# ScalarE's addition in the linear attention's queries: queued with the reduction, or as an item of its own

## The chip, the cores and the metric

The kernel runs on one core of a Trainium2 chip. A core has five engines, each with an in-order queue of its own: TensorE (PE; its weight loads, PEld, overlap its matmuls), VectorE (DVE), ScalarE (ACT), GpSimd (POOL) and SyncE (SP, which issues the DMAs here). They wait for one another by semaphores. An instruction that waits also holds whatever stands behind it on its engine. The metric is the device time of one execution in microseconds (us), the median of the runs shown.

## The reference

Two attention blocks on the same input x (2048 tokens, 1024 columns, 32 heads of 32 columns), mixed by a gate. Block A is linear attention, block B softmax attention:

```python
phi = lambda t: jnp.where(t > 0, t + 1, jnp.exp(t)) + 1e-6
pq, pk = phi(q), phi(k)                       # block A
kv = jnp.einsum("bhsd,bhse->bhde", pk, v)
z = jnp.einsum("bhsd->bhd", pk)
num = jnp.einsum("bhqd,bhde->bhqe", pq, kv)
den = jnp.einsum("bhqd,bhd->bhq", pq, z)[..., None] + 1e-6
a = (num / den) @ wo
...
p = _softmax(q @ k * Dh ** -0.5)              # block B, per head
b = (p @ v) @ wo
...
g = _sigmoid((x * gate_w).sum(-1, keepdims=True))
return g * a + (1 - g) * b
```

The constant 1e-6 that is added to `den` is the subject of the change.

## The kernel before, in words

All products in float32 are made of three matmuls of a high and a low part (lines 147 to 149). After a first phase that computes block B's values, queries and keys, four streams share the engines. They are Python generators, and a planner in the kernel's source runs them and so writes out the order of every engine's queue by hand:

- `maxima` (block B): for each head, 64 score tiles of 128 x 512 on PE (L890), whose row maxima VectorE takes (L895); at a head's end these are turned into two rows (`mh`, `ml`) and stored by DMA beside the head's queries.
- `heads_` (block B): the scores again, transposed (L1041), their exponentials on ScalarE (L1045), their product with the values on PE in groups of 5, 5 and 6 tiles (L1139), and their sums on GpSimd (L1092, L1088) and VectorE (L1099, L1101). L943 and L950 to L953 end a head.
- `linear` (block A): units of 128 tokens by 512 columns, 24 matmuls each (L147 to L149), in the order values (of block B), keys and values, queries, output product. The queries have two chunks of 16 units, so 32 units.
- `output`: the last products, the gate and the mixture.

The planner keeps a clock for each engine, `T["pe"]`, `T["act"]`, `T["dve"]`, `T["pool"]`. `use(engine, cost, *after)` moves an engine's clock to the latest of its own time and the times given, adds a planned cost, and returns the end with a latency. An instruction is put into its engine's queue at the moment at which the planner runs the Python line, so the order of these calls is the order of the queue. VectorE's work is mostly deferred: `defer` makes an item with a due time `at`, and `fill(until)` runs those that fit before `until`, which reaches 0.4 us, or, between score tiles, 1.2 us, past PE's planned time. `run` computes an item's planned end before it calls the item's function with that end. `take()` gives out one of six PSUM banks and runs the deferred readers that still hold it. `tasks` is a list of pairs (start, function): in each round of the main loop the first task whose start is no later than PE's planned time is run ahead of the streams.

A unit of the queries: after its matmuls, ScalarE makes the exponential, the positive part and a sum (`phi`, L567 to L569). Then a chain of four items on VectorE: `sums` (L799) and `scaled` (L802, times the keys' sums `zrep`), `dens` (L807, a reduction over each head's 32 columns to the 128 x 16 tile `dn`) and `divide` (L812 a reciprocal, L813 the product with it). `dens` also issues ScalarE's addition of the constant to `dn` (L808) and sets the due time of `divide`, which is `last[0]`. After `divide` a task, `queries`, transposes the result on PE (L693), ScalarE copies it rounded (L695), VectorE takes the remainder (L698) and two DMAs store both (`oA`, L700), on SP's queue, where the loads of later rows (`xs`, L562) and of block B's heads (L861) stand as well.

Of the kernel before, what the change touches and what calls it, by code (L numbers as in the profile page):

```python
# [46 lines left out]
def kernel(  # L47
# [19 lines left out]
    nc = tc.nc  # L67
# [39 lines left out]
    eps = sb.tile([P, 1], F32, name="eps")  # L107
# [47 lines left out]
    def use(eng, cost, *after):  # L155

        T[eng] = max(T[eng], *after, 0.0) + cost
        return T[eng] + LATENCY[eng]
# [35 lines left out]
    def ended(items, *also):  # L194

        if any(item.end is None for item in items):
            return None
        return max([0.0, *also] + [item.end for item in items])
# [19 lines left out]
    def take():  # L218

        idle = [b for b in RING if not held[b]]  # L220
        times = {b: ended(readers[b], free[b]) for b in idle}
        b = min(idle, key=lambda b: (times[b] is None, times[b] or 0.0))
        need(readers[b])
        free[b] = ended(readers[b], free[b])
        readers[b].clear()
        held[b] = True
        return b
# [77 lines left out]
    def xop(name, p, i):  # L305
        return big[XO[name][p]][:, i * C:(i + 1) * C]
# [126 lines left out]
    for np_, js in enumerate(PAIRS):  # L433
# [4 lines left out]
        for pos, k in enumerate(KORDER):  # L438
# [3 lines left out]
            for t in range(2 * TPC):  # L442
# [3 lines left out]
                ps = bank[t]  # L446
# [14 lines left out]
        for g in range(NK):  # L461
            nxt = pair_ops(g + 1) if g + 1 < NK else None
            for q, name in enumerate(PRODUCTS):
                ps = bank[used % 8]
# [165 lines left out]
    def load_mix():  # L630
        while stores:
            stores.popleft()()
        a, c = mix_todo.popleft()
        for i in range(HK):
            nc.sync.dma_start(mix_hi[i], a_wo[(a * HK + i) * P:(a * HK + i + 1) * P, c * C:(c + 1) * C])
        mix_here.append((a, c, T["pe"] + MIX_LAND))
# [70 lines left out]
    def linear():  # L707
        extra = iter(())
        coming_w = deque()
        for n, (i, t) in enumerate(units):  # L710
            kind, c = chunks[i]
            pos = n % NT
            here_ = n < NT // 2
            follow = chunks[i + 1] if i + 1 < len(chunks) else None
            xp = xp_t[n % 2]
            yield bank_at
            b = take()
            ps = bank[b]
            T["pe"] = max(T["pe"], free[b])
            lin_kind[0] = kind  # L720
            if kind in ("q", "o") and c == 0 and t in (2, 8, NT - 2):
                yield lambda: None if mix_here else 0.0
                if t < NT - 2:
                    load_mix()
                while stores:
                    stores.popleft()()
            if n < 2:
                load_head(n)
                load_v(n)
            for k in range(NK):  # L730
                yield lambda: ended(w_left[k], w_ready[k], 0.0 if here_ else xp_ready[n % 2])
                need(w_left[k])
                if here_:
                    jj, tt = divmod(n, TPC)
                    stat = [xop(PLACE[jj][k // HK], p, k % HK)[:, tt * P:(tt + 1) * P] for p in range(2)]
                else:
                    stat = [blocks(xp, p)[:, k] for p in range(2)]
                for m, _ in enumerate(three(ps, stat, (wpart(k, 0), wpart(k, 1)), k)):
                    lin_pe(1.0)
                    if m < 2:  # L740
                        yield always
                if k == 0 and n + 7 == len(units) and not o_main[0]:
                    load_o(0)
                if k == 1 and n + 1 == len(units):
                    split_o(0, slice(0, NK - 1))
                if k == NK // 2 and n + 1 == len(units) and over["head"]:
                    split_o(1, slice(0, NK - 1))
                if k == NK - 1:
                    yield from extra
                if follow and follow[0] == "o":  # L750
                    if pos == NT - 1:
                        w_left[k].clear()
                        yield lambda: 0.0 if mixed.count((k // HK, follow[1])) == 8 else None
                        load_wa(follow[1], k)
                    continue
                if kind == "v":
                    if pos == (NT - 4 if k < NK // 2 else NT - 3):
                        coming_w.append(load_w(*follow, k, LEAD_W + 1, first_raws[k]))
                elif follow and pos == NT - 2 and k < min(LEAD_W, NK):
                    coming_w.append(load_w(*follow, k, LEAD_W + 1))  # L760
                if follow and pos == NT - 1:
                    split_w(*follow, k, *coming_w.popleft(), nc.vector if kind == "v" else nc.gpsimd)
                    if kind != "v" and k + LEAD_W < NK:
                        coming_w.append(load_w(*follow, k + LEAD_W, LEAD_W + 1))
            if NT // 2 <= n + 2 < len(units):
                load_xp(n + 2)
            extra = iter(())
            e, r = mid[3 + n % 3], mid[6]
            if kind == "v":
                give(b, use("act", 0.5, T["pe"] + LATENCY["pe"]))  # L770
                v_out(c, t, ps, mid[(10, 11, 7, 8, 9)[n % 5]])
            elif kind == "kv":
                va = mid[7][:, (n % 2) * HC:(n % 2 + 1) * HC]
                yield from keys_alone(n - 2)
                nc.scalar.copy(va, ps[:, HC:])
                use("act", 0.28, T["pe"] + LATENCY["pe"])
                end = phi(ps, e, HC)

                def more(end, c=c, t=t, e=e, ps=ps):
                    pk = e[:, :HC]  # L780
                    nc.vector.scalar_tensor_tensor(pk, pk, 1.0, ps[:, :HC], op0=ALU.min, op1=ALU.add)
                    z_end[c % 2] = use("pool", 0.69, end)
                    if t == 0:
                        nc.gpsimd.tensor_copy(zsum[c % 2], pk)
                    else:
                        nc.gpsimd.tensor_add(zsum[c % 2], zsum[c % 2], pk)

                todo = [defer(more, end, 0.34)]
                give(b, 0.0, todo)
                keys(n, c, t, e, va, todo)  # L790
                if t == NT - 1:
                    extra = keysum(c)
            elif kind == "q":
                yield lambda: None if n - 3 not in turned and chunks[units[n - 3][0]][0] == "q" else 0.0
                end = phi(ps, e, C)
                d = dn[n % 2]

                def sums(_, e=e, ps=ps):
                    nc.vector.scalar_tensor_tensor(ps, e, 1.0, ps, op0=ALU.min, op1=ALU.add)  # L799

                def scaled(_, c=c, ps=ps, r=r):
                    nc.vector.tensor_mul(r, ps, zrep[:, c * C:(c + 1) * C])  # L802

                last = []

                def dens(end, r=r, d=d, last=last):
                    nc.vector.tensor_reduce(d, r.rearrange("p (h d) -> p h d", d=DH), AX.X, ALU.add)  # L807
                    nc.scalar.add(d, d, eps)  # L808
                    last[0].at = use("act", 0.2, end)

                def divide(_, t=t, e=e, ps=ps, d=d):
                    nc.vector.reciprocal(d, d)  # L812
                    nc.vector.tensor_mul(  # L813
                        e.rearrange("p (h d) -> p h d", d=DH), ps.rearrange("p (h d) -> p h d", d=DH),
                        d.unsqueeze(2).to_broadcast([P, C // DH, DH]))

                todo = chain(((sums, 0.63), (scaled, 0.63), (dens, 0.63), (divide, 0.9)), end)
                last.append(todo[-1])
                give(b, 0.0, todo)
                tasks.append((lambda todo=todo: both(ended(todo + o_left), bank_at()),  # L820
                              lambda n=n, c=c, t=t, e=e, todo=todo: queries(n, c, t, e, todo)))
            else:
                res = mid[14 if c == 0 and t < TPC else (14, 8)[n % 2]]
                give(b, use("act", 0.5, T["pe"] + LATENCY["pe"]))
                nc.scalar.copy(res, ps)
                nc.sync.dma_start(ra_d[t][:, c * C:(c + 1) * C], res)
        over["lin"] = True
        load_all()
# [9 lines left out]
    tasks = []  # L838
# [25 lines left out]
    def load_head(h):  # L864
        load_q(h)
        for j in range(NJ):
            load_k(h, j)
# [4 lines left out]
    def load_v(h):  # L872
        c, o = divmod(h * DH, C)
        nc.sync.dma_start(v_tile(h), v_d[c][:, :, o:o + DH])
# [537 lines left out]
```

## Time and profile before

| | |
|---|---|
| median of 3 runs | 2850.99 us (2850.79 to 2853.78) |
| the profiled execution | 2850.77 us, of it 2849.0 us span from first to last instruction |
| busy: PE, weight loads, VectorE, ScalarE, GpSimd | 100%, 71%, 79%, 57%, 65% of the span |
| mean granted TensorE clock | 0.999 |
| the queries' additions (L808) | 32, from 1722.4 to 2133.9 us |

The times of the trace are counted from the first instruction. PE's records are those of pipelined matmuls with modelled ends, so they overlap, and a PE that is shown as busy may still pause briefly: the distance from start to start tells more. An idle time is put down to the event that ended it, and idle time of an engine that is not the bottleneck costs nothing.

### The profile page before, as it was taken

Reading aid. Unit: us, or ns where it says so; the run is one execution under the profiler, and the core shown is the slowest. Engines: PE = TensorE matmul, PEld = TensorE weight load, DVE = VectorE, ACT = ScalarE, POOL = GpSimd, SP = SyncE. Lnnn points to the kernel's source line nnn. Section 1 sums busy time; section 2 is a strip of 40 time slices with the busy share of each in tenths; the row PEclk is TensorE's granted clock in tenths of the full one; section 3 lists DMA queues with packets and bytes.
Section 4 is the critical chain, followed back from the end, with each engine's and each line's share of the span. In section 5 each row is a group of like instructions: output and inputs, shape, how many; then the busy total and the mean of one; then the engine's idle time right before and its main releaser. Section 6 shows DMA issues by size and latency. Waiting matters only on the chain.

```text
span 2849.0 us, 44413 instructions
## 1 busy us (share of the span) xinstructions
PE 2836.9 (100%) x15744; PEld 2033.4 (71%) x15744; DVE 2238.1 (79%) x3775; ACT 1617.8 (57%) x3007; POOL 1854.5 (65%) x646
## 2 busy tenths in 40 slices
PE   9999999999999999999999999999999999999999
PEld 7888888766666666666666667676766666666787
DVE  6666656888888888888888888888988778886743
ACT  5334320666666667666666666675656566656421
POOL 1212220778898889988988888687778777875000
PEclk9999999999999999999999999999999999999999
DMA  5956865432333223332323234574464444424663
GB/s 166 295 170 207 263 192 165 125 94 92 109 90 93 90 89 110 93 103 90 122 79 93 90 119 149 182 219 141 145 199 140 125 141 136 141 85 147 220 213 105
DMA packets 302498, 400.57 MB, mean 141 GB/s; under 512 B 92682, under 2 KB 185354, under 8 KB 299146
## 3 DMA queue, kind: packets, MB, share of 16 engines
q1 hardware_dynamic: 302276, 397.73, 45.3%
q8 instruction: 124, 2.03, 0.3%
q14 instruction: 98, 0.80, 0.1%
HBM read 287.57 MB, written 108.79 MB: 139 GB/s over the span
## 4 chain that ended last, share of the span: by engine, by line
PE 95%; DMA 2%; DVE 2%; issue 1%; ACT 1%; POOL 0%; SPq 0%; POOLq 0%; ACTq 0%
PE bank L1041 17%; PE bank L890 16%; PE bank L1139 15%; PE bank L147 11%; PE bank L149 11%; PE bank L148 11%; PE bank L410 3%; PE bank L409 3%; PE bank L408 3%; PE bank L943 1%; DMA mid<-in_xT 1%; PE bank L693 1%; PE bank L449 1%; PE bank L448 1%; PE bank L447 1%
## 5 line engine op out<-in xcount | busy, mean ns | idle before, releaser
L1092 POOL TENSOR_TENSOR big<-big,big 128x1536 f32<-128x1536 f32 (+1 forms) x434 | 1557.2, 3588 | 184.6 <-ACT big L1045 162.2
L895 DVE TENSOR_REDUCE mx<-bank 128x1 f32<-128x512 f32 x2048 | 1311.1, 681 | 315.5 <-PE bank L890 311.3
L1045 ACT ACTIVATE big<-bank 128x512 f32<-128x512 f32 x2048 | 1181.2, 601 | 517.5 <-PE bank L1041 449.5
L1041 PE MATMUL bank<-big,big 128*128 128x512 f32 x2048 | 808.9, 397 | 2.4 <-DMA big<-ml 2.3
L890 PE MATMUL bank<-big,big 128*128 128x512 f32 x2048 | 802.4, 392 | 0.3 <-ACT big L1045 0.3
L147 PE MATMUL bank<-big,big 128*128 128x512 f32 x1408 | 551.7, 392 | 2.9 <-ACT big L253 1.7
L149 PE MATMUL bank<-big,big 128*128 128x512 f32 x1408 | 550.1, 391 | 0.7 <-DVE big L254 0.4
L148 PE MATMUL bank<-big,big 128*128 128x512 f32 x1408 | 550.3, 391 | 0.0
L1041 PEld LDWEIGHTS bank<-big,big 128*128 128x128 f32 x2048 | 383.8, 188 | 158.5 <-issue 64.7
L1139 PE MATMUL bank<-big,mid 128*32 128x512 f32 x4096 | 460.8, 595 | 0.0
L890 PEld LDWEIGHTS bank<-big,big 128*128 128x128 f32 x2048 | 384.6, 188 | 84.5 <-ACT big L1045 4.3
L1139 PEld LDWEIGHTS bank<-big,mid 128*32 128x32 f32 x4096 | 127.8, 110 | 265.2 <-issue 265.2
L147 PEld LDWEIGHTS bank<-big,big 128*128 128x128 f32 x1408 | 264.3, 188 | 66.1 <-ACT big L1045 5.9
L149 PEld LDWEIGHTS bank<-big,big 128*128 128x128 f32 x1408 | 264.3, 188 | 57.5 <-DVE big L254 0.8
L148 PEld LDWEIGHTS bank<-big,big 128*128 128x128 f32 x1408 | 264.4, 188 | 55.2
L1101 DVE TENSOR_TENSOR bank<-bank,big 128x512 f32<-128x512 f32 (+1 forms) x434 | 280.5, 646 | 6.8 <-ACT big L1045 5.5
L1088 POOL TENSOR_TENSOR big<-big,big 128x1536 f32<-128x1536 f32 (+1 forms) x31 | 111.6, 3602 | 235.6 <-ACT big L1045 123.7
L254 DVE TENSOR_TENSOR big<-mid,big 128x512 fp32r<-128x512 f32 x216 | 153.2, 732 | 84.1 <-ACT big L253 84.0
L387 POOL TENSOR_TENSOR mid<-mid,mid 128x512 f32<-128x512 f32 x16 | 20.7, 1291 | 277.6 <-DVE big L254 266.3
L253 ACT CAST big<-mid 128x512 fp32r<-128x512 f32 x216 | 130.2, 624 | 97.9 <-POOL mid L388 54.5
L410 PE MATMUL bank<-big,big 128*128 128x512 f32 x448 | 174.4, 389 | 0.1
L408 PE MATMUL bank<-big,big 128*128 128x512 f32 x448 | 174.4, 389 | 0.0
(103 smaller groups left out, 1977.3 us busy)
## 6 DMA issues: line engine op xcount, KB each, us to landing
big<-xs SPq DMA_DIRECT2D x208, 512.0 KB
qk<-mid SPq DMA_DIRECT2D x128, 256.0 KB
big<-oA SPq DMA_DIRECT2D x64, 512.0 KB
big<-qk SPq DMA_DIRECT2D x96, 256.0 KB
big<-qk SPq DMA_DIRECT2D x384, 64.0 KB
mid<-in_b_wqkv SPq DMA_DIRECT2D x88, 256.0 KB
xs<-big SPq DMA_DIRECT2D x64, 256.0 KB
oA<-mid SPq DMA_DIRECT2D x64, 256.0 KB
```

The lines of the kernel that those rows point to most:

```text
L147: yield nc.tensor.matmul(ps, sh, mh_, start=(kt == 0), stop=False)
L148: yield nc.tensor.matmul(ps, sh, ml_, start=False, stop=False)
L149: yield nc.tensor.matmul(ps, sl, mh_, start=False, stop=(kt == NK - 1))
L408: nc.tensor.matmul(ps, sh, mh_, start=(i == 0), stop=False)
L410: nc.tensor.matmul(ps, sl, mh_, start=False, stop=(i == HK - 1))
L890: nc.tensor.matmul(bank[b], q[:, t * P:(t + 1) * P], k[:, j * C:(j + 1) * C], start=True, stop=True)
L895: nc.vector.tensor_reduce(m[:, t, j:j + 1], bank[b], AX.X, ALU.max)
L1041: nc.tensor.matmul(bank[b], k[:, t * P:(t + 1) * P], q[:, j * C:(j + 1) * C], start=True, stop=True)
L1045: nc.scalar.activation(pr_t[i][:, j * C:(j + 1) * C], bank[b], AF.Exp, scale=SCALE)
L1092: nc.gpsimd.tensor_add(lacc[:, :qp], lacc[:, :qp], pr(t)[:, :qp])
L1101: nc.vector.tensor_add(lacc[:, qp:] if t == NT - 1 else l_b[:, :n], l_b[:, :n], src)
L1139: nc.tensor.matmul(av_b[j * DH:(j + 1) * DH, :], v[:, t, :], pr(t)[:, j * C:(j + 1) * C], start=(t == 0), stop=(t == NT - 1))
```

## The change

In the version before, `dens` puts the reduction into VectorE's queue and at once the addition into ScalarE's queue. In the changed version `dens` issues the reduction only, gives `divide` the due time end + 0.6, and makes a function `plus` that issues the addition. `plus` becomes a task that starts at the reduction's planned end, so it enters ScalarE's queue when PE's planned time has come to there. When it runs it sets the due time of `divide` anew from ScalarE's planned time. If `divide` is run before that (when its bank is wanted, say), it calls `plus` first; `plus` takes itself out of `last`, so that it is issued once.

```diff
                 def dens(end, r=r, d=d, last=last):
                     nc.vector.tensor_reduce(d, r.rearrange("p (h d) -> p h d", d=DH), AX.X, ALU.add)
-                    nc.scalar.add(d, d, eps)
-                    last[0].at = use("act", 0.2, end)
-
-                def divide(_, t=t, e=e, ps=ps, d=d):
+                    last[0].at = end + 0.6
+
+                    def plus():
+                        if plus in last:
+                            last.remove(plus)
+                            last[0].at = use("act", 0.2, end)
+                            nc.scalar.add(d, d, eps)
+
+                    last.append(plus)
+                    tasks.append((lambda: end, plus))
+
+                def divide(_, t=t, e=e, ps=ps, d=d, last=last):
+                    for fn in last[1:]:
+                        fn()
                     nc.vector.reciprocal(d, d)
                     nc.vector.tensor_mul(
```

## The prediction, made before the changed kernel had run

> **What bounds the kernel now.** I read the page first: the engines' busy time and the chain that ended last.
>
> ```profile
> PE 2836.9 (100%) x15744; PEld 2033.4 (71%) x15744; DVE 2238.1 (79%) x3775; ACT 1617.8 (57%) x3007; POOL 1854.5 (65%) x646
> PE 95%; DMA 2%; DVE 2%; issue 1%; ACT 1%; POOL 0%; SPq 0%; POOLq 0%; ACTq 0%
> ```
>
> TensorE is 95% of the chain, ScalarE 1%. The edit concerns only the stage with the linear attention's queries, so I next took the busy times by stage: the stretch before (linear attention's keys), the stretch of the queries, the last stretch (output products only). The columns are the stretch, its length, then busy us of PE, PE's weight loads, VectorE, ScalarE, GpSimd, the granted clock, DMA share and GB/s.
>
> ```profile
> 1300.00:1715.00 415.00, 415.00 (x2567) 283.34 (x2568) 354.79 (x603) 273.90 (x531) 365.30 (x132) 1.00 0.33 99
> 1720.00:2140.00 420.00, 418.40 (x2301) 294.14 (x2300) 363.76 (x636) 266.58 (x506) 318.92 (x85) 1.00 0.55 175
> 2700.00:2849.00 149.00, 145.13 (x641) 119.84 (x639) 56.62 (x136) 28.42 (x37) 0.00 (x0) 1.00 0.51 164
> ```
>
> In the queries' 420 us PE is recorded idle for 420 - 418.40 = 1.6 us. ScalarE has 420 - 266.58 = 153 us idle, VectorE 56. Third, the instructions on the tile of the denominators, `dn`, with what they waited for:
>
> ```profile
> L808 ACT ACTIVATE dn<-dn,eps x32: 307/308/340, 1722.4 to 2133.9; 128x16 f32<-128x16 f32 x32
> L812 DVE RECIPROCAL dn<-dn x32: 194/241/253, 1723.5 to 2135.3; 128x16 f32<-128x16 f32 x32
> its engine sat idle before it (us, times) until:
>   DVE dn L807: 32.2, 29
>   ACT dn L808: 0.4, 1
> who waited for it (us, times):
> ...
>   PEld bank L693: 0.8, 1
> ```
>
> So there is something to remove: at 29 of 32 additions ScalarE stood idle, 32.2 us in all, 1.1 us each, until VectorE's reduction ended. VectorE waited for the addition only once, 0.4 us. Fourth, one such stall in order of time, with PE's records before and after it (start, length, engine, line):
>
> ```profile
> 2104.19 0.39 PE L1041 MATMUL bank<-big,big 128*128 128x512 f32 x1
> ...
> 2105.57 0.68 DVE L807 TENSOR_REDUCE dn<-mid 128x16 f32<-128x512 f32 x1
> ...
> 2106.28 0.31 ACT L808 ACTIVATE dn<-dn,eps 128x16 f32<-128x16 f32 x1 [1.06 <-DVE dn L807]
> ...
> 2106.49 1.07 ACT L1045 ACTIVATE big<-bank 128x512 f32<-128x512 f32 x2
> ...
> 2108.29 0.24 DVE L812 RECIPROCAL dn<-dn 128x16 f32<-128x16 f32 x1
> ...
> 2108.95 0.39 PE L890 MATMUL bank<-big,big 128*128 128x512 f32 x1
> ```
>
> The two PE rows are the first and the last of 22 consecutive 512-column matmuls: 4.76 us for 21 steps, 0.2267 us a step, straight through a ScalarE stall of 1.06 us. Matmul records overlap (0.39 long, 0.2267 apart), so a short pause could hide in "busy"; the step shows that here none did. Behind the stall two exponentials that had been held ran back to back in 1.07 us.
>
> **The change part by part.** No instruction is added or removed: 32 reductions, 32 additions, 32 reciprocals and multiplications stay, on the same engines, with the same waits. What moves is the addition's place in ScalarE's queue: behind the exponentials that are issued between the planner's emission of the reduction and the planned end of the reduction. Each part in turn.
>
> *ScalarE's stall.* 32.2 us of idle time go, if the planner's time of the end is right. Those exponentials start up to 1.1 us sooner. What are they worth to the end? They free PSUM banks for PE. PE's waits in this stretch, and its weight loads' waits for exponentials:
>
> ```profile
> PE bank L147 <- DMA big<-xs: 1.2, 1, 1.2
> PE bank L890 <- ACT big L1045: 0.3, 1, 0.3
> ...
> PEld bank L147 <- ACT big L1045: 3.7, 11, 1.6
> PEld bank L890 <- ACT big L1045: 1.9, 6, 0.7
> PEld bank L1041 <- ACT big L1045: 1.1, 4, 0.3
> ```
>
> Lower bound of the gain: 0.3 us, the one matmul that waited for an exponential. Upper bound: all weight loads that did, 3.7 + 1.9 + 1.1 = 6.7 us, though a weight load runs ahead of its matmul and its wait need not reach it. I take 0.3, the row of the matmuls themselves, because the step of 0.2267 us is unbroken at the stall shown. What is late next on ScalarE is PE itself:
>
> ```profile
> ACT big L1045 <- PE bank L1041: 57.3, 105, 6.5
> ```
>
> ScalarE already waits 57.3 us for PE's scores; most of the 32.2 us should reappear there, as idle time of another name.
>
> *The addition and what follows it.* It now stands behind the exponentials that used to be held. At the stall shown these are two, 1.07 us, and the idle time was 1.06 us: they fit into the gap, and the addition would start about when it does now. Where one more exponential has begun, it is later by up to 0.60 us (1.07 / 2 rounded up), and so is the reciprocal. At worst 32 x 0.6 = 19 us of lateness are spread over the stage, at best none. On VectorE nothing stands still for it: the planner gives divide a due time of at least the reduction's end plus 0.6 and lets row maxima go first, as it does now (the reciprocal above starts 1.7 us after the addition ended). Cost taken: 0. If that cover is gone, VectorE pays the 0.4 us that the one wait of today shows, for each of the 32 units at worst 13 us, against its 56 us of idle time.
>
> *Behind divide.* The transposes of the queries, ScalarE's rounded copy, VectorE's remainder and two stores on SP's queue all wait for divide; the bank of the product is held as long. A unit is 420 / 32 = 13 us of PE time, and the next use of the same buffer is three units on. The transposes' weight load waited for divide once, 0.8 us, and the matmul not at all. Cost taken: 0.
>
> *SP's queue.* The stores of a unit (L700) stand ahead of later loads in it, and it is held by them today:
>
> ```profile
> SPq L700 <- ACT mid L695: 58.0, 17, 7.6
> ```
>
> Lateness of divide of up to 0.6 us adds at most 19 us to this; the only load that PE felt here is the row `xs` above, 1.2 us. Cost taken: 0; this is the slower rival.
>
> *The plan's clock.* Without the addition pushing the planned ScalarE time to the reduction's end, the planner orders the later streams differently. PE's amount of work does not change by it. What may change is whether PE runs into a late transfer. The nearest such event lies right after the stage; the last two rows are the same group of 48 matmuls, after the wait and undisturbed, and the clock of 8 us from the wait on:
>
> ```profile
> 2211.05 0.47 PE L1041 MATMUL bank<-big,big 128*128 128x512 f32 x1 [2.32 <-DMA big<-ml]
> ...
> 2211.97 6.92 PE L1139 MATMUL bank<-big,mid 128*32 128x512 f32 x48
> ...
> 2278.29 5.29 PE bank L1139 x48
> ...
> 2211.00:2219.00 8.00, 7.96 (x52) 2.30 (x53) 0.69 (x1) 0.60 (x2) 3.17 (x1) 0.79 0.54 175
> ```
>
> One such event costs 2.32 + (6.92 - 5.29) = 3.95 us, since the granted clock fell to 0.79. It may vanish (-3.95) or a second may come (+3.95); I take 0 and keep both in the range. [...]
>
> **The sum.** The profiled execution took 2850.77 us, a span of 2849.0 and 1.77 around it; it lies 0.2 under the median of 2850.99. 2850.77 - 0.3 + 0 + 0 + 0 = 2850.5 us. A change of 0.2%, 5.7 us, is about what can be told from none here.
>
> **The rivals.** *Faster: PE was held by the exponentials after all.* Price: 6.7 us, giving 2844.1; it decides if 5.7 of the 6.7 come back. To see whether so much is there I add up the stretch:
>
> ```profile
> L1041 PE MATMUL bank<-big,big 128*128 128x512 f32 x322 | 127.8, 397 | 0.1
> L890 PE MATMUL bank<-big,big 128*128 128x512 f32 x321 | 127.1, 397 | 0.3 <-ACT big L1045 0.3
> L147 PE MATMUL bank<-big,big 128*128 128x512 f32 x255 | 100.6, 395 | 1.2 <-DMA big<-xs 1.2
> L148 PE MATMUL bank<-big,big 128*128 128x512 f32 x255 | 100.0, 392 | 0.0
> L149 PE MATMUL bank<-big,big 128*128 128x512 f32 x255 | 99.7, 391 | 0.0
> L1139 PE MATMUL bank<-big,mid 128*32 128x512 f32 x640 | 72.1, 594 | 0.0
> L693 PE MATMUL bank<-ident,mid 128*128 128x128 f32 x128 | 19.7, 276 | 0.0
> L943 PE MATMUL bank<-big,ones 128*32 128x512 f32 x40 | 5.3, 604 | 0.0
> ...
> 2083.25 0.44 PE bank L693 x4
> 2092.56 0.99 PE bank L943 x8
> 2093.55 4.29 PE bank L1139 x40
> ```
>
> 1408 x 0.2267 = 319.2; 640 / 40 x 4.29 = 68.6; 128 / 4 x 0.44 = 14.1; 40 / 8 x 0.99 = 5.0; together 406.9 of 420. So 13.1 us remain for smaller groups, switches between kinds of matmul and every pause: 6.7 fits in it, but the switches of 16 groups of L1139 and 32 of transposes are in it too, and they stay. [...] Chance 0.10.
>
> *Slower: SP's queue hands the lateness on.* If divide is late by 0.6 us in every unit, the stores hold SP longer, the next `xs` rows come late and PE waits for them as in the row of 1.2 us. If half the lateness reached PE: 32 x 0.3 = 9.6 us, giving 2860.4. It decides from 5.7 / 32 = 0.18 us a unit. Against it: one such wait in 32 units today, with stalls of the same size in play, and the two exponentials that fit the gap. Chance 0.09.
>
> *The wait mostly stays.* The planner's clock gives the reduction 0.63 us where the row has 0.68; VectorE is 363.76 / 420 = 87% busy and may run behind the plan, so that the addition, queued at the planned end, again stands ahead of the real one. Then half, some 16 us, of idle time stays at L808, and the time is 2850.8. Chance 0.21.
>
> **How the numbers follow.** The forecast, stall gone and nothing gained, has 0.60; with the wait that stays 0.81 is no change. Faster 0.10, slower 0.09. The range goes from 2844.1 (the weight loads' bound) to 2850.77 + 3.95 = 2854.7 (one more late transfer), which leaves out the slower rival and part of the faster one.
>
> **What would show it.** Right: L808's idle time under 10 us; ScalarE's wait for L1041 up by some 20 us from 57.3; PE busy in the stretch between 417 and 420 of 420 and the stage as long as now, about 32 units of 13 us; the reciprocal later by under 1 us. Wrong: weight loads' waits for L1045 gone and the stage shorter by 5 us or more (faster), or new waits of L147 for `xs` (slower). The forecast fails too if the new order makes or removes more than one late transfer anywhere behind the stage.

## The result, and the profile after

The changed kernel took 2867.55 us (median of 6 runs, 2863.29 to 2869.92) against 2851.26 (2850.79 to 2853.78) for the kernel before on the same chip: a ratio of 1.0051 [1.004, 1.0062], 16.3 us slower. The forecast of 2850.5 and its range up to 2854.7 are missed. The profiled execution took 2867.08 us, a span of 2865.3; the span before was 2849.0, so this one trace holds all of the 16.3 us. Behind line 809 lines are numbered 10 higher than before: L814 is the addition, L822 the reciprocal, L900 and L1051 the two kinds of score matmuls, L1055 the exponential, L1157 ScalarE's copy at a head's end.

The change did what it says. These are the rows of the tile `dn` over the stage, now 1720 to 2160 us:

```profile
L814 ACT ACTIVATE dn<-dn,eps x32: 297/300/342, 1723.1 to 2151.1; 128x16 f32<-128x16 f32 x32
L822 DVE RECIPROCAL dn<-dn x32: 193/240/253, 1726.2 to 2152.2; 128x16 f32<-128x16 f32 x32
...
  DVE dn L807: 7.2, 4
  ACT dn L814: 6.0, 2
...
  PE bank L693: 2.5, 2
```

ScalarE's idle time ahead of the addition fell from 32.2 us in 29 places to 7.2 in 4. But the reciprocal now waited 6.0 us for the addition (0.4 before), and TensorE's transposes L693 waited 2.5 us for what follows (0 before). The stage by busy times (columns as before: length, PE, weight loads, VectorE, ScalarE, GpSimd, clock, DMA share, GB/s), over the same stretches as in the prediction:

```profile
1300.00:1715.00 415.00, 415.00 (x2566) 283.09 (x2566) 354.44 (x603) 273.40 (x530) 365.76 (x133) 1.00 0.33 99
1720.00:2140.00 420.00, 407.18 (x2228) 285.50 (x2227) 349.04 (x609) 256.44 (x483) 306.42 (x82) 0.98 0.52 166
```

The keys' stretch is as it was. In the queries' 420 us PE has 407.18 us busy instead of 418.40, at a clock of 0.98 instead of 1.00. The waits of the stage (1720 to 2160; who waited for whom, total, times, longest):

```profile
ACT big L1055 <- PE bank L1051: 78.6, 173, 4.4
...
PE bank L1051 <- ACT big L1055: 10.1, 3, 5.9
ACT mid L695 <- DMA oA<-mid: 9.8, 2, 6.6
...
DVE dn L822 <- ACT dn L814: 6.0, 2, 4.1
...
PE bank L693 <- DVE mid L823: 2.5, 2, 2.0
```

Two rows are new: ScalarE's rounded copy L695 waits twice for a store of `oA` to land, and PE waits 10.1 us for exponentials (0.3 us before, once). The larger of the two places in time, ScalarE, SP and PE (SPq rows are the issue of DMAs):

```profile
1815.22 9.72 SPq L635 DMA_DIRECT2D big<-in_a_wo  x4
...
1826.13 0.39 PE L149 MATMUL bank<-big,big 128*128 128x512 f32 x1
1827.27 1.24 SPq L700 DMA_DIRECT2D oA<-mid  x2
...
1831.30 0.59 ACT L695 CAST mid<-bank 128x512 fp32r<-128x512 f32 x1 [6.56 <-DMA oA<-mid]
1831.78 1.09 ACT L1055 ACTIVATE big<-bank 128x512 f32<-128x512 f32 x2
...
1832.44 0.79 PE L1051 MATMUL bank<-big,big 128*128 128x512 f32 x1 [5.92 <-ACT big L1055]
...
1833.46 0.63 PE L1051 MATMUL bank<-big,big 128*128 128x512 f32 x1
1833.88 0.63 PE L147 MATMUL bank<-big,big 128*128 128x512 f32 x1
```

Read it from the top. SP issues four loads of `a_wo` (L635, the block that `load_mix` fetches at the start of units 2 and 8) and is held by them from 1815.22 to 1824.94. The stores of unit 6 stand behind them and leave at 1827.27. They read the copy's buffers `oh` and `ol` (`mid[8]`, `mid[9]`), of which there is one pair for all units. So the copy of unit 7 waits 6.56 us until the store has landed; the exponentials stand behind the copy in ScalarE's queue; PE, with no bank free, stops for 5.92 us. Then its matmuls start 0.42 us apart (1833.46 to 1833.88) instead of 0.2267. The same stretch of SP before the change:

```profile
1808.14 0.86 SPq L700 DMA_DIRECT2D oA<-mid  x2
...
1812.28 8.89 SPq L635 DMA_DIRECT2D big<-in_a_wo  x4
```

There the stores stood ahead of the loads and left 4 us before them; the changed plan runs `queries` just behind `load_mix` instead of just ahead of it. The other place, at 1736.64, is of the same kind, with unit 0 and the first block of `a_wo`:

```profile
1726.91 1.83 SPq L635 DMA_DIRECT2D big<-in_a_wo  x4
...
1731.07 2.25 SPq L700 DMA_DIRECT2D oA<-mid  x2
...
1738.47 0.59 ACT L695 CAST mid<-bank 128x512 fp32r<-128x512 f32 x1 [3.22 <-DMA oA<-mid]
...
1739.61 0.50 PE L1051 MATMUL bank<-big,big 128*128 128x512 f32 x1 [2.58 <-ACT big L1055]
```

Here the loads held SP for 1.83 us only, but the copy could start no sooner than 7.4 us after the first store had left (1731.07 to 1738.47), against 4.0 us at the larger place (1827.27 to 1831.30). Why this store took longer to land is not shown; e4 below takes the loads out from ahead of it, and the wait is gone. The third pause is of another kind:

```profile
1996.34 0.68 DVE L807 TENSOR_REDUCE dn<-mid 128x16 f32<-128x512 f32 x1
...
2001.52 0.59 ACT L1157 COPY mid<-bank 128x512 f32<-128x512 f32 x1 [5.58 <-PE bank L1149]
2002.00 0.31 ACT L814 ACTIVATE dn<-dn,eps 128x16 f32<-128x16 f32 x1
2002.34 0.25 DVE L822 RECIPROCAL dn<-dn 128x16 f32<-128x16 f32 x1 [4.13 <-ACT dn L814]
...
2003.46 1.05 PE L693 MATMUL bank<-ident,mid 128*128 128x128 f32 x4 [2.02 <-DVE mid L823]
```

The reduction ended at 1997.02, but the addition now stands behind ScalarE's copy at a head's end, which waits 5.58 us for a group of PE's products. The reciprocal is 4.13 us late and the transposes hold PE for 2.02 us. The clock around the three places:

```profile
1736.00:1745.00 9.00, 6.42 (x21) 4.68 (x20) 4.21 (x8) 3.94 (x8) 1.06 (x1) 0.81 0.75 180
1826.00:1837.00 11.00, 5.08 (x15) 3.76 (x14) 3.43 (x6) 3.57 (x7) 0.00 (x0) 0.69 0.98 238
2001.00:2007.50 6.50, 4.48 (x20) 3.40 (x14) 2.83 (x5) 2.48 (x5) 0.00 (x0) 0.74 0.93 182
```

From start to start of PE's matmuls the three places cost this much. First: a gap of 2.97 - 0.23 = 2.74 us, then a step of 0.397 and seven of 0.427, 1.6 us more than eight of 0.2267, together 4.3. Second: 6.31 - 0.23 = 6.08, and steps of 0.592, seven of about 0.427 and one of 0.353 behind it, 1.9, together 8.0. Third: 2.02, transposes of 1.05 instead of 0.66, and steps of 0.574 and five of 0.427, 1.35, together 3.8. 4.3 + 8.0 + 3.8 = 16.1 us, against 16.3 in all. That they meet so closely is in part chance, for elsewhere in the two traces gains and losses cancel: PE's wait for `ml` behind the stage (2.00 us at 2226.99) no longer cost it its clock, and its wait of 1.21 us for `xs` is gone; but a pause of 1.56 us came at 1927.84, and one of 1.71 us at 2684.80 (1.66 before) now did cost the clock.

### The profile page after: what moved, and what is told of

The parts are those of the page before. It is cut to its first block, busy times and chain, and to the rows that moved or that the text cites. A ratio compares the mean times of both kernels' runs of the same rounds, so it can differ in the third digit from the quotient of the medians.

```text
span 2865.3 us, 44410 instructions
## 1 busy us (share of the span) xinstructions
PE 2842.6 (99%) x15744; PEld 2039.1 (71%) x15744; DVE 2237.8 (78%) x3775; ACT 1620.3 (57%) x3007; POOL 1854.8 (65%) x646
## 5 line engine op out<-in xcount | busy, mean ns | idle before, releaser
L1055 ACT ACTIVATE big<-bank 128x512 f32<-128x512 f32 x2048 | 1184.4, 602 | 536.1 <-PE bank L1051 470.1
L1051 PE MATMUL bank<-big,big 128*128 128x512 f32 x2048 | 811.6, 398 | 12.1 <-ACT big L1055 10.1
L900 PE MATMUL bank<-big,big 128*128 128x512 f32 x2048 | 803.8, 392 | 0.0
L147 PE MATMUL bank<-big,big 128*128 128x512 f32 x1408 | 553.5, 393 | 2.0 <-ACT big L253 1.7
L149 PE MATMUL bank<-big,big 128*128 128x512 f32 x1408 | 552.0, 392 | 0.5 <-DVE big L254 0.4
L1051 PEld LDWEIGHTS bank<-big,big 128*128 128x128 f32 x2048 | 384.9, 188 | 169.5 <-issue 63.6
L900 PEld LDWEIGHTS bank<-big,big 128*128 128x128 f32 x2048 | 385.4, 188 | 83.5 <-ACT big L1055 3.6
L147 PEld LDWEIGHTS bank<-big,big 128*128 128x128 f32 x1408 | 265.2, 188 | 65.5 <-ACT big L1055 5.6
L149 PEld LDWEIGHTS bank<-big,big 128*128 128x128 f32 x1408 | 265.5, 189 | 57.5 <-DVE big L254 0.8
```

The lines of the kernel that those rows point to most:

```text
L147: yield nc.tensor.matmul(ps, sh, mh_, start=(kt == 0), stop=False)
L149: yield nc.tensor.matmul(ps, sl, mh_, start=False, stop=(kt == NK - 1))
L900: nc.tensor.matmul(bank[b], q[:, t * P:(t + 1) * P], k[:, j * C:(j + 1) * C], start=True, stop=True)
L1051: nc.tensor.matmul(bank[b], k[:, t * P:(t + 1) * P], q[:, j * C:(j + 1) * C], start=True, stop=True)
L1055: nc.scalar.activation(pr_t[i][:, j * C:(j + 1) * C], bank[b], AF.Exp, scale=SCALE)
```

## The experiments

Ratios are against the kernel before, on the same chip (medians there 2850.51 to 2851.08); they are estimated over the runs and need not be the quotient of the medians shown. Names of the parts: *order* is the new order of all queues that the changed plan gives; *addition* its new place on ScalarE; *own tiles* and *ahead of the copy* are two cures told below.

| run | what | median us | ratio [95%] |
|---|---|---|---|
| e1 | order, addition back behind the reduction | 2870.47 | 1.0068 [1.0055, 1.008] |
| e2 | order of before, addition moved on ScalarE | 2855.09 | 1.0014 [1.0005, 1.0022] |
| e3 | changed kernel, own tiles | 2858.62 | 1.0026 [1.0016, 1.0036] |
| e4 | changed kernel, `a_wo` loads behind the stores | 2860.68 | 1.0029 [1.0018, 1.004] |
| e5 | kernel before, own tiles | 2849.29 | 0.9998 [0.9989, 1.0007] |
| e6 | e2, addition ahead of the copy | 2849.47 | 0.9997 [0.9988, 1.0006] |
| e7 | e3, addition ahead of the copy | 2855.87 | 1.0017 [1.0009, 1.0026] |
| e8 | kernel before, addition on VectorE | 2901.04 | 1.0176 [1.0162, 1.019] |
| e9 | kernel before, two stores behind the `a_wo` loads | 2862.18 | 1.0041 [1.0028, 1.0054] |
| e10 | e9, own tiles | 2849.61 | 0.9996 [0.9987, 1.0005] |
| e11 | e6, own tiles | 2849.99 | 0.9999 [0.999, 1.0008] |
| e12 | e7, `a_wo` loads behind the stores | 2855.43 | 1.0018 [1.001, 1.0027] |
| e13 | e7, one row `xs` ahead of two stores | 2853.7 | 1.0011 [1.0002, 1.002] |
| e14 | e7, one row `xs` behind `a_wqkv` | 2854.61 | 1.0008 [0.9999, 1.0017] |
| e15 | e13 and e14 | 2851.89 | 1.0003 [0.9994, 1.0011] |

**Which half of the change?** e1 keeps every queue in the changed order and puts the 32 additions back to where they stood on ScalarE; e2 keeps every queue of before and moves only the additions.

```diff
 e1, against the changed kernel
+                    nc.scalar.add(d, d, eps)
                     last[0].at = end + 0.6
...
-                            nc.scalar.add(d, d, eps)
 e2, against the changed kernel
-                    last[0].at = end + 0.6
+                    last[0].at = use("act", 0.2, end)
...
-                            last[0].at = use("act", 0.2, end)
                             nc.scalar.add(d, d, eps)
```

> All engines' queues as in the changed kernel, except that the 32 additions stand again where the reduction is issued. Store theory (ScalarE's rounded copy L695 waits for the DMA that still reads its only buffer, because the changed plan puts the unit's stores behind four loads of a_wo on SP's queue): the copies and the stores stay where they are, so 2862 to 2868 us. Rival, the late addition itself (reciprocal and transposes wait for it): 2850 to 2853. Rival, PE's new order by itself: 2862 to 2868.

> All engines' queues as in the kernel before, except that the 32 additions stand later on ScalarE, at the planned end of the reduction. Store theory: the order on SP is the old one, so 2849 to 2853 us, L814's idle time far under the 32.2 us of before and nothing gained by it. Rival, the late addition itself: 2862 to 2868. Rival, PE's new order: 2849 to 2853.

e1 has the stall of ScalarE back and all of the loss; its waits over 1720 to 2160:

```profile
ACT dn L808 <- DVE dn L807: 32.2, 30, 2.2
...
PE bank L1051 <- ACT big L1055: 8.1, 6, 4.8
ACT mid L695 <- DMA oA<-mid: 6.9, 2, 5.5
```

So most of the loss is in the order of the other queues, and comes with or without the stall. e1 lost 19.4 us, more than the change did, although its copies waited less for stores (6.9 against 9.8 us); what the rest of its loss is was not followed up. e2 has the stall gone (6.8 us left in 4 places) and still loses 4 us, which neither side of its expectation had. PE has two new waits there, one of 1.2 us for an exponential and this one:

```profile
DVE dn L821 <- ACT dn L813: 3.0, 3, 2.5
...
PE bank L693 <- DVE mid L822: 2.0, 1, 2.0
```

That is the third kind of pause, at another head's end (1733 us). 2.0 us and the slow steps behind it (0.35 + 6 x 0.2 = 1.55) are 3.6 of the 4.

**Is it the store and the single buffer?** e3 takes the buffer away: the copy goes into the unit's own product tile, which the transposes have just read, and the remainder alternates between two tiles. The order of every queue stays. e4 leaves the buffer and takes away the lateness: the `a_wo` loads wait on SP's queue until the unit's stores have been issued. e5 is the first edit on the kernel before.

```diff
 e3, e5
-    oh, ol = f32r(mid[8]), f32r(mid[9])
...
-        nc.scalar.copy(oh, pt)
+        oh, ol = f32r(pq), f32r(mid[8 + n % 2]); nc.scalar.copy(oh, pt)
 e4, in load_mix and behind the unit's stores
+        go = lambda: [nc.sync.dma_start(mix_hi[i], ...) for i in range(HK)]
+        late.append(go) if lin_kind[0] == "q" else go()
...
+            [late.pop()() for _ in list(late)]
```

> The changed kernel with the same order on every engine, but the rounded copy goes to the unit's own tile (three take turns) and the remainder to one of two, so no copy has to wait for the unit before's store. Store theory: the two pauses of PE of 2.7 and 6.1 us and the slow clock behind them (1.6 and 2.0 us) go, 2867.5 - 12.4 = 2855 us, and the wait of ScalarE's L695 for oA is gone. Rival, the late addition: 2862 to 2868. Rival, PE's new order: 2862 to 2868.

> The changed kernel with one thing moved: on SP's queue two blocks of four loads of a_wo stand behind the unit's two oA stores instead of ahead of them. All other queues are the same row by row. Store theory: the second and larger pause (6.1 us and 2.0 us of slow clock) goes and the first (2.7 and 1.6) mostly, 2855 to 2859 us. Rivals, the late addition or PE's new order: 2862 to 2868.

> The kernel before, its order kept on every engine, with the unit's own tile for the rounded copy and two for the remainder. Store theory: no copy waits for a store here, so there is nothing to win, 2849 to 2853 us. Rival, the single buffer costs in every order: 2845 or less.

In e3 the copy never waits for `oA`, and 8.9 of the 16.3 us are back. That is less than the 12.3 us of the two places: PE now waited for `xs` near 1836 (1.5 and 0.5 us), which in the changed kernel it did nowhere in the stage. In e4 the first place is gone; at the second the store was still 4.8 us short of landing:

```profile
PE bank L1051 <- ACT big L1055: 6.3, 2, 4.2
...
ACT mid L695 <- DMA oA<-mid: 4.8, 1, 4.8
```

e4 is only half a cure, and its time is between, 1.7 us above its expected range. e5 shows that the tiles by themselves are worth nothing that can be measured: what they repair in e3 came with the new order.

**Is it enough to make the loss?** e9 takes the kernel before and changes SP's queue alone: the stores of units 0 and 6 go behind the `a_wo` loads. e10 does so with own tiles.

```diff
 e9
-            for p, src in enumerate((oh, ol)):
-                nc.sync.dma_start(oA_d[p][t][:, ...], ...)
+            go = lambda: [nc.sync.dma_start(oA_d[p][t][:, ...], ...) for p, src in enumerate((oh, ol))]
+            late.append(go) if c == 0 and t in (0, 6) else go()
 e9, at the end of load_mix
+        [late.pop()() for _ in list(late)]
```

> The kernel before with one thing changed: on SP's queue the oA stores of units 0 and 6 stand behind the four loads of a_wo instead of ahead of them; all other queues the same row by row. Store theory (this order and the single buffer are enough): ScalarE's copy of units 1 and 7 waits for the stores by some 3 and 6 us, PE stands still behind it and loses its clock, 2857 to 2865 us. Rival, the cost needs the changed plan or the late addition: 2849 to 2853.

> The same swap on SP's queue, and the rounded copy has the unit's own tile, the remainder one of two. Store theory: the late stores hurt nobody, 2848 to 2853 us. Rival, the order on SP costs by itself (late xs loads, more DMA traffic at once): as the swap alone, 2857 to 2865.

The waits of e9:

```profile
ACT mid L695 <- DMA oA<-mid: 10.0, 2, 6.4
PE bank L1041 <- ACT big L1045: 9.3, 3, 5.8
```

Two stores behind two blocks of loads make 11.7 us (2862.18 against 2850.51) and the very waits of the changed kernel (9.8 and 10.1 us there); with own tiles the same queue costs nothing. The mechanism is shown from both sides, and it is 4.3 + 8.0 of the loss in the trace of the changed kernel.

**The late addition.** In e6, e7 and e11 an addition that is still pending is issued ahead of ScalarE's copy at a head's end.

```diff
+                for fn in list(hurry):
+                    fn()
                 nc.scalar.copy(avs, av_b)
```

> As the version with the old plan and late additions (2855.1), but an addition that is still pending is put ahead of ScalarE's copy at a head's end, which waits there some 5 us for TensorE's group; all other queues the same. Theory of the late addition (at that one place it makes reciprocal, product and transposes late: 2.0 us and the slow clock behind it): 2850.5 to 2852, PE's wait of L693 for the product gone. Rival (the 4 us are something else, spread over the 32 additions): 2854 to 2856.

> The changed kernel with both: own tiles for copy and remainder, and pending additions ahead of the copy at a head's end. Theory: of the 2858.6 of the own tiles alone the wait of the transposes (2.0 us) and its slow clock (1.6) go, 2855 us or a little under. If these two causes were all, 2851 to 2853. Rival, PE's new order has a cost of its own: 2856 to 2859.

> The old plan, the additions at the planned end of the reduction but ahead of the copy at a head's end, and own tiles for copy and remainder: everything found so far that costs nothing. If ScalarE's 32 us were worth something it would be here: 2846 or less. Theory (worth nothing measurable): 2848 to 2851.

e6 against e2: the transposes' wait and the whole of the 4 us are gone. e11 is the change with both faults cured in the order of before: the stall of ScalarE is down to 9.1 us in 5 places, and the ratio is 0.9999 [0.999, 1.0008]. Taking the stall away is worth nothing here that this interval, 3 us to either side, could show. e7 cures both faults in the new order and still is slow.

**The last 5 us.** e12 adds e4's cure to e7.

> The changed kernel with all three cures: own tiles, additions ahead of the copy at a head's end, and a_wo's loads behind the unit's stores. Theory that the rest of the loss (2855.9 with two cures) is the order on SP, where loads of xs stand late: 2851 to 2854. Rival, the rest is PE's new order: 2855 to 2858.

It did nothing more, so late stores were no longer the matter. By its expectation that speaks for the rival, a cost of PE's new order; the next runs test it. Its profiled execution (2859.44 us, above the median) shows what was next in line:

```profile
PE bank L147 <- DMA big<-xs: 3.7, 1, 3.7
...
ACT big L550 <- DMA big<-in_a_wqkv: 2.9, 2, 2.4
...
PE bank L1058 <- ACT big L1062: 1.8, 1, 1.8
```

Two more transfers late on SP's queue: a row `xs` behind the stores of unit 7, which held SP for 6.16 us, and a load of `a_wqkv` behind another row `xs`, for which a cast of ScalarE waits, with exponentials behind it. e13 puts these stores behind that `xs`, e14 the other `xs` behind three loads of `a_wqkv`, e15 does both; nothing else moves on any queue.

```diff
 e13, in low (queries), flushed at the end of load_xp
+            held_st.append(go) if c == 0 and t == 7 else go()
 e14, in load_xp, flushed behind the last load of a_wqkv
+        held_x.append(go) if kind == "q" and chunks[i][1] == 1 and t == 0 else go()
```

> The changed version with the own tiles and the addition ahead of the copy, and on SP alone the two stores of the unit 7 of the first chunk put behind the load of the row xs that follows them; PE, VectorE, ScalarE and GpSimd keep their order. Theory 'the last 5 us are two late transfers' (xs behind the store of unit 7 with a pause of up to 4 us, and ScalarE's cast that waits 2 us for a_wqkv): no wait for xs at 1830 to 1840, 2852.5 to 2854.5. Rival 'the last 5 us are spread over many small pauses of the new order': 2855 to 2856.5.

> The changed version with the own tiles and the addition ahead of the copy, and on SP alone the load of one row xs (for the first unit of the second chunk) put behind three loads of a_wqkv that stood behind it. Two late transfers: ScalarE's cast no longer waits for a_wqkv, 2853 to 2855. Spread pauses: 2855 to 2856.5. If the moved xs itself is late at the first unit of the second chunk, PE waits for it and the time is 2857 or more.

> Both moves on SP together. Two late transfers: 2850 to 2852, the time of the kernel before. Spread pauses: 2855 to 2856.5.

In e13 PE no longer waits for `xs` at L147 (0.7 us are left at L149) and the cast still waits. In e14 the cast no longer waits, and PE waits for `xs` at two places, one of them that of the row that was moved (1.3 us at 1918.20). First a fence of e13, then one of e14:

```profile
ACT big L550 <- DMA big<-in_a_wqkv: 3.0, 1, 3.0
...
PE bank L1058 <- ACT big L1062: 2.5, 1, 2.5
```

```profile
PE bank L147 <- DMA big<-xs: 1.9, 2, 1.2
PE bank L149 <- DMA big<-xs: 1.8, 2, 1.3
```

With both moves the time is 2851.89 us and can't be told from that of the kernel before. e13 and e14 each stand between, 1.3 to 2.2 us under e7, which singly is less than the intervals can separate; the step from e7 to e15 is 4.0 us, with intervals that still overlap a little (from 1.0009, up to 1.0011). So the rest was probably late transfers too, of the two kinds that the traces name. PE's new order has no cost of its own beyond e15's interval, for e15 keeps it. No version was faster than the kernel before by more than its interval.

**A way round ScalarE, which failed.** e8 takes the addition off ScalarE: VectorE does it itself behind the reduction, all other queues as before.

```diff
-                    nc.scalar.add(d, d, eps)
+                    nc.vector.tensor_scalar_add(d, d, 1e-6)
```

> The kernel before, every order kept, but the 32 additions are done by VectorE right behind the reduction, at 0.16 us each or 5 us in all, and ScalarE has none. Theory (ScalarE's 32 us of standing still were worth nothing, PE set the time): 2849.5 to 2852 us with ScalarE's wait for L1041 up by about 30 us. Rival, the stall was worth PE time: 2845 or less. Rival, VectorE is the bound: 2855 or more.

It took 50 us more than before. The 32 additions were expected to take 0.16 us each; by the tile `dn` and in one place in time:

```profile
L808 DVE TENSOR_SCALAR dn<-dn x32: 174/1852/3366, 1721.1 to 2182.6; 128x16 f32<-128x16 f32 x32
```

```profile
1875.46 4.03 POOL L1092 TENSOR_TENSOR big<-big,big 128x1792 f32<-128x1792 f32 x1 [0.34 <-ACT big L1045]
1875.64 0.68 DVE L807 TENSOR_REDUCE dn<-mid 128x16 f32<-128x512 f32 x1
1876.35 3.16 DVE L808 TENSOR_SCALAR dn<-dn 128x16 f32<-128x16 f32 x1
1879.43 0.68 DVE L895 TENSOR_REDUCE mx<-bank 128x1 f32<-128x512 f32 x1
```

The addition ends at 1879.51, right behind GpSimd's sum that was running (1879.49); the reduction L807 in the midst of the same sum took its usual 0.68. By the row above half of the 32 additions took 1.85 us or more. Where no sum was running (one had ended at 1788.84, the next began at 1796.01), an addition took 0.17 us, as little as any:

```profile
1784.79 4.05 POOL L1092 TENSOR_TENSOR big<-big,big 128x1792 f32<-128x1792 f32 x1 [1.03 <-ACT big L1045]
...
1789.15 0.17 DVE L808 TENSOR_SCALAR dn<-dn 128x16 f32<-128x16 f32 x1
...
1796.01 4.06 POOL L1092 TENSOR_TENSOR big<-big,big 128x1792 f32<-128x1792 f32 x1 [7.17 <-ACT big L1045]
```

Row maxima stand behind it, and PE waited 30.3 us for them in 17 places, which before was no row at all.

## Why the prediction was wrong, step by step

- *ScalarE's stall*: right. The 32.2 us went (7.2 left, under the 10 forecast), reappeared as waiting for PE's scores (57.9 to 78.6 us over 1720 to 2160; 78.8 in e11, where none of the three pauses is), and were worth nothing (e11). The forecast gain of 0.3 us did not come either: a wait of 0.3 us for an exponential is in the new trace too. The faster rival, PE held by the exponentials, is refuted by e11.
- *The addition and what follows it*: mis-sized. It bounded the lateness of one addition by one exponential, 0.6 us. What else stands in ScalarE's queue was not looked through: the copy at a head's end waits up to 5.58 us for PE, and the addition behind it made divide 4.13 us late. Cost taken 0, measured 3.8 us in the changed kernel and 4 us in e2, each time in one place.
- *Behind divide*: the step that failed. It let the transposes, the copy, the remainder and the stores be late, since "the next use of the same buffer is three units on". That is true of the product's tile. The copy's own buffers are one pair for all units, and what frees them is a DMA on SP's queue. The next unit's copy waits for that DMA in front of all exponentials. Cost taken 0; the two pauses are 12.3 us by the trace, 11.7 by e9.
- *SP's queue*: the right queue and the wrong victim. Lateness was to add up evenly, 0.3 us in each of 32 units, and to reach PE through `xs`. What happened is that the new plan moved the stores of two units behind blocks of loads: a change of order, which is a step and not a slope. (The loads held SP for 9.72 us at one place and 1.83 at the other.) In the changed kernel PE waited for `xs` nowhere in the stage; it did so, for 3.7 us, once the rest had been cured (e12). The slower rival had the sign, and with 9.6 us some three fifths of the size, but by a mechanism that did not happen.
- *The plan's clock*: the price of one event, 3.95 us, fits the new ones (3.8 and 4.3, and 8.0 for the long one), but not the event it was taken from: the same wait for `ml` was 2.00 us in the changed kernel and left the clock at 1.00. That one event at most would come or go was wrong: three came, and they came inside the stage, where none was looked for. The new order of all queues should have been costed as several draws of this kind, with a range beyond one event above.
- *The wait mostly stays*: refuted by the row of L814.

Of the marks named beforehand, L808's idle time and ScalarE's longer wait for PE's scores came as forecast; PE's busy time (407.18, not 417 to 420 of 420) and the reciprocal's lateness (4.13, not under 1 us) showed the forecast wrong.

## What to carry to other kernels

When a step is made later, follow each of its buffers to the instruction that frees it, and that instruction to its place in its own queue: a single buffer that a queued store must free ties two in-order engines together (11.7 us in e9). Removing idle time of an engine that wasn't the bound brought nothing here, while reordering a tightly planned schedule can bring several late transfers; count them as a number of events with a price, not as one. The price is the pause, and sometimes the slow matmuls behind it (3.8, 4.3 and 8.0 us at the three places of the changed kernel).

## What the runs showed of the hardware

A short pause of PE can halve its clock, but its length alone does not tell whether it will. In e12 a wait of 1.79 us was followed by 3.41 us at a granted clock of 0.50, with matmuls 0.427 us apart. In the changed kernel a wait of 2.00 us left the clock at 1.00. First two rows of e12, then two of the changed kernel:

```profile
1920.87 0.50 PE L1058 MATMUL bank<-big,big 128*128 128x512 f32 x1 [1.79 <-ACT big L1062]
```

```profile
1921.46:1924.87 3.41, 3.15 (x8) 2.41 (x8) 1.41 (x3) 2.90 (x6) 3.41 (x3) 0.50 0.85 309
```

```profile
2226.99 0.47 PE L1051 MATMUL bank<-big,big 128*128 128x512 f32 x1 [2.00 <-DMA big<-ml]
```

```profile
2227.00:2235.00 8.00, 8.00 (x59) 3.45 (x60) 1.54 (x3) 2.28 (x4) 3.44 (x1) 1.00 0.57 181
```

In the traces of the kernels before and after, from 60 us on, PE has nine waits of 1 us or more. Those of 1.21 and 1.66 us (before, at 1835.04 and 2670.06) and of 1.56 and 2.00 us (after, at 1927.84 and 2226.99) left the clock at 1.00. Those of 2.32 us (before, at 2211.05) and of 1.71, 2.02, 2.58 and 5.92 us (after) came with a clock of 0.50. It lasted 6.83 us at the longest of them and 3.41 us at the others. First the row of before, then four of after:

```profile
2211.77:2215.18 3.41, 3.41 (x17) 0.80 (x20) 0.69 (x1) 0.43 (x1) 2.40 (x1) 0.50 0.66 207
```

```profile
1740.70:1744.11 3.41, 3.41 (x10) 2.64 (x9) 2.28 (x4) 1.44 (x4) 0.00 (x0) 0.50 0.87 200
1829.45:1836.28 6.83, 3.84 (x9) 3.07 (x10) 3.00 (x5) 3.37 (x6) 0.00 (x0) 0.50 1.07 205
2003.53:2006.94 3.41, 3.41 (x11) 2.83 (x12) 1.54 (x3) 1.68 (x3) 0.00 (x0) 0.50 0.98 154
2686.19:2689.60 3.41, 3.41 (x9) 2.65 (x9) 3.27 (x6) 0.00 (x0) 0.00 (x0) 0.50 0.70 220
```

In e12 a wait of 3.74 us came with 0.50 over the whole of 1836.60 to 1842.00. Even the same wait can differ: the transposes' wait of 2.0 us cost the clock in the changed kernel and not in e3, whose profiled execution had a mean granted clock of 1.000. So one trace can show such a pause as 1.35 or 1.6 us dearer than the next one does (the slow steps at the third and the first place above): e3's profiled execution took 2852.99 us, the fastest of its nine, 5.6 us under their median.

A VectorE addition of 128 x 16 elements took 3.16 us beside a sum of GpSimd and 0.17 us where none was running (e8; 0.17 to 3.37 us over all 32), while the reductions L807 (0.66 to 0.69 us) and the products L813 (0.69 us) kept their time. The addition of 3.16 us ended 0.02 us behind the sum; what holds it is not shown. The expectation of e8 had taken 0.16 us for every addition and had nothing on GpSimd's sums.
